# Block-sparse attention and a Fourier mixer on one core: another order of table loads and last stores, and one round of the second channel layer as seven block products

## The chip, the core and the metric

The kernel runs on one core of a Trainium2 chip. A core has five engines that run side by side, each with its own instruction stream: TensorE (PE) multiplies matrices from SBUF into PSUM, VectorE (DVE) and ScalarE (ACT) work on tiles elementwise, GpSimd (POOL) does the same more slowly, and SyncE (SP) here does little but issue DMA transfers, in its order. Data is held in SBUF (128 partitions); products land in PSUM, which has 8 banks. The engines meet by semaphores: an instruction whose input isn't there waits, and all that stands behind it on its engine waits with it.

The metric is the device time of one execution in microseconds (us). Of the kernel before, three runs are shown.

## The reference

The input has 4 batches, 8 heads, 768 positions and 64 numbers per head. The first part is attention with a mask by blocks of 32 positions: a block sees its neighbours, the first and last block, all blocks if it is itself the first or last, and three sampled ones.

```
scores = scale * q @ k.T                 # per batch and head, 768 x 768
scores = where(mask, scores, -1e9)
attn   = exp(scores - max) / (sum + 1e-9)
o      = attn @ v                        # 768 x 64
x      = o, heads side by side           # (4, 768, 512)
```

The second part mixes x by Fourier transforms and two channel layers:

```
u  = x + real(fft(fft(x, axis=1), axis=2))
un = (u - mean(u)) / sqrt(var(u) + 1e-6)
y  = u + relu(un @ w_ch1) @ w_ch2        # 512 -> 2048 -> 512
```

The weights arrive as float64; x and y are float32.

## The kernel before

All work is in float32. For each batch there are four pairs of heads (`NP` = 4), so 16 pairs in all. The work for a pair is cut into six steps called slots (`slot(sl)`, `SP` = 6); a phase is one batch's 24 slots (`SB` = 24), and there are 96 slots in all. In a slot, TensorE makes two tiles of scores (`scores`, L578: s, transposed, keys on partitions), ScalarE exponentiates them (`weigh`, L598 or L606), for the tiles whose mask is not made by TensorE VectorE multiplies by the mask (L608), and TensorE multiplies by v one or two slots later (`values`, L652: o, transposed). The sums for the softmax are gathered on GpSimd and VectorE (L638). When the six slots of one half of the positions are through, `place` transposes the result (xt, L673 to L676: three TensorE transposes and one copy by ScalarE) into x, or `place_blocks` sends it through HBM. x has two halves, xA and xB (384 positions each: tiles 0 to 2 and 3 to 5 of 128), with two buffers each, so batch b's x takes the buffer of batch b-2: it can't be written before b-2's result, which lies there, has been stored.

Which position lies in which partition of which tile is given by the table `_ORDER`: each row names a tile, a first partition, how many tiles and rows, and the first position and its step. The loads of q, k and the sine table and the stores of the output follow it; one DMA is issued for each row.

The mixer of batch b-1 runs inside the attention of batch b; that of the last batch runs behind all attention. Its parts, in order: `fourier` folds x, multiplies by the cosine and sine tables of the positions (zp, L860) and then by those of the channels (`across`, pq, L891 to L908); `arrive` adds the result to x; `spread` takes mean and variance (VectorE's statistics L941, GpSimd's root L943 to L945); `whiten` makes un (L955). un is needed transposed: in batches 0 to 2 VectorE transposes blocks of 32 (`un_blocks`, L1014), the rows go to HBM (far<-un) and come back in another order (unT<-far, `fetch`, L1027); in the last batch TensorE transposes (`un_flip`, utp, L996).

The channel layers then run in rounds; four rounds of 512 hidden channels each for batches 0 to 2. A round has two calls of `quad`, which makes two strips of 128 hidden channels by two halves of positions with 7 block products instead of 8 (xp, yp and z at L1103; the combined operands `right`, L1065, and `left`, L1085; sums L1108; relu L1112; the hidden layer lies in hA and hB), and six calls of `channels`: for each half and each tile of 128 positions, four matmuls of 512 columns (y, L1159) and one addition into x (L1162). In the last round the finished x is stored (`store`, L1170). The last batch has two rounds of 1024 hidden channels, in each four quads and then `outputs` for the tiles in the order `OUT`: tile m of xA and tile m of xB are made together by 7 block products (yy, L1224) with sums of operands (`output_left`, `output_right`) and additions (L1231, L1254).

The order of all this is written by a planner in Python that runs before the kernel does. It keeps a model clock for each engine (`when`, moved on by `busy(engine, us, after)`) and for each PSUM bank (`free`). Work that belongs to attention is emitted by `slot`; the mixer's steps wait in queues: `apart` (the Fourier part, normalisation, operands of the first quad), `late` (quads and channels, each with a price in us) and `short` (small TensorE steps that need one bank). `gap` emits from `apart` what the model clocks say fits in now. `until(met)` emits `late` and `apart` until a condition holds; it is used where x's buffer must be free (`finished` holds the halves whose stores have been issued) and at the end, for the last batch. In `slot`, for the first pair of a phase from phase 2 on (`reuse`), the place of the first half stands at step s >= 5 and first calls `until` for batch b-2's half; the placing itself is emitted in the next slot behind its scores and exponentials (`state["place"]`).

At the start the weights are loaded in 32 pieces (`w_load`, L456, by SP) and rebuilt from float64 by two ScalarE and five VectorE instructions each (`w_round`, L465 to L477). Six steps for the Fourier tables are spread over the slots by `table_step`: each step loads a table into one of two buffers (tab, L391 for the positions' tables) and later copies it in its final order with VectorE (L397). From slot 4 on, every even slot loads one and, from the third on, first copies out the oldest:

```
if len(table_put) == 2 or not table_steps:
    if table_put:
        table_put.popleft()()
if table_steps:
    fn, args = table_steps.pop(0)
    get, put = fn(*args)
    get()
    table_put.append(put)
```

A second version of the whole kernel (`general`) stands behind a condition for scores too large to be exponentiated without their maximum; it is not executed with these inputs.

## Time and profile before

| what | us |
|---|---|
| median of 3 runs | 1051.01 (1050.29 to 1051.64) |
| the profiled execution | 1051.83 |
| its span, first to last instruction | 1049.9 |
| TensorE busy | 1022.6 (97%) |
| VectorE busy | 672.5 (64%) |
| ScalarE busy | 356.2 (34%) |
| GpSimd busy | 236.6 (23%) |
| mean granted clock of TensorE | 0.994 of full speed |

How to read the rows of the profile. Times are us from the start of the span. In a row of the timeline stand the start, the duration, the engine, the line of the kernel, the operation, the output and inputs with partitions x elements, and how many like instructions were joined in the row; a bracket at the end gives the idle time ahead of it and what ended that. "SPq" is SP's queue for issuing DMAs and "ACTq" that of ScalarE; a DMA row's duration is the time for issuing, not for the transfer. A float32 matmul is recorded as two parts, so the x8 behind y stands for four matmuls. In a table by stretches of time, a row holds the stretch, its length, then busy time and count for PE, PEld, DVE, ACT and POOL, then the granted clock of TensorE, the mean busy share of the 16 DMA engines and the GB/s moved. In the chain of waits, a row names the waiting queue or engine, the one it waited for with the line, the time in all, how often and the longest.

### The profile page before, as it was taken

How to read it: one execution, taken by the hardware profiler on the slowest of the kernel's cores; microseconds unless marked ns; L12 is line 12 of the kernel's file. 1: busy time of each engine (PE TensorE's matmuls, PEld its weight loads, DVE VectorE, ACT ScalarE, POOL GpSimd, SP SyncE). 2: the span in 40 equal slices, each digit the busy share in tenths (PEclk: the TensorE clock that was granted, in tenths of full speed). 3: DMA queues.
4: the chain of work that ended last, by engine and by line, in shares of the span. 5: the costliest groups of instructions: out<-in, count | busy, mean ns of one | idle time of the engine just before them, and what ended most of it. 6: DMA issues, size and time to landing. Idle time of an engine off the chain costs nothing. (4 is left out here: it accounts for less than half of the span.)

```text
span 1049.9 us, 12342 instructions
## 1 busy us (share of the span) xinstructions
PE 1022.6 (97%) x4350; PEld 530.7 (51%) x4350; DVE 672.5 (64%) x1232; ACT 356.2 (34%) x718; POOL 236.6 (23%) x264
## 2 busy tenths in 40 slices
PE   8999999999999999999999999899999999999996
PEld 4333345444465554444444654444445654578585
DVE  6898885977845844655578467565558364774663
ACT  6979756554020112432441211243221111210210
POOL 1000074655000100554553001256420001000000
PEclk9999999999999999999999999999999999999998
DMA  7757522282000035232220003721010001000001
GB/s 212 227 180 216 121 47 46 51 140 37 1 1 20 31 40 87 62 64 39 56 58 1 1 10 74 124 53 42 16 25 7 0 1 39 22 1 1 1 17 46
DMA packets 163455, 58.05 MB, mean 55 GB/s; under 512 B 144172, under 2 KB 154170, under 8 KB 163386
## 3 DMA queue, kind: packets, MB, share of 16 engines
q1 hardware_dynamic: 162134, 56.45, 24.1%
q10 hardware_dynamic: 1220, 0.72, 0.3%
q8 instruction: 36, 0.59, 0.2%
q14 instruction: 33, 0.27, 0.1%
q0 software_dynamic: 32, 0.01, 0.0%
HBM read 43.80 MB, written 13.37 MB: 54 GB/s over the span
## 5 line engine op out<-in xcount | busy, mean ns | idle before, releaser
L638 POOL TENSOR_TENSOR acc<-acc,e 128x384 f32<-128x384 f32 x156 | 159.2, 1054 | 90.6 <-DVE e L608 68.2
L578 PE MATMUL s<-qT,kT 64*128 64x384 f32 x768 | 154.0, 515 | 9.8 <-ACT e L598 8.4
L652 PE MATMUL o<-e,vr 128*64 128x384 f32 x768 | 142.9, 499 | 0.0
L1159 PE MATMUL y<-w_sb,hB 128*128 128x512 f32 x288 | 128.1, 595 | 0.3 <-DVE x L1162 0.3
L1159 PE MATMUL y<-w_sb,hA 128*128 128x512 f32 x288 | 127.9, 595 | 0.0
L1162 DVE TENSOR_TENSOR x<-y,x 128x512 f32<-128x512 f32 x72 | 49.7, 690 | 113.8 <-PE y L1159 113.4
L608 DVE TENSOR_TENSOR e<-s,mask 128x768 f32<-128x768 f32 x84 | 76.3, 950 | 54.5 <-ACT s L606 46.3
L578 PEld LDWEIGHTS s<-qT,kT 64*128 64x128 f32 x768 | 63.7, 185 | 90.6 <-ACT e L598 29.0
L638 POOL TENSOR_TENSOR acc<-e 128x384 f32<-128x384 f32 x42 | 48.0, 1164 | 249.7 <-ACT e L598 125.6
L606 ACT ACTIVATE s<-s 128x768 f32<-128x768 f32 x84 | 63.6, 792 | 113.9 <-PE s L578 113.7
L598 ACT ACTIVATE e<-s 128x768 f32<-128x768 f32 x108 | 82.6, 812 | 56.0 <-PE s L588 35.0
L1103 PE MATMUL z<-unT,t 128*128 128x384 f32 x256 | 93.5, 488 | 0.0
L1159 PEld LDWEIGHTS y<-w_sb,hB 128*128 128x128 f32 x288 | 53.4, 190 | 66.5 <-issue 65.2
L1159 PEld LDWEIGHTS y<-w_sb,hA 128*128 128x128 f32 x288 | 53.7, 190 | 63.7 <-issue 60.0
L652 PEld LDWEIGHTS o<-e,vr 128*64 128x64 f32 x768 | 48.0, 137 | 69.7 <-issue 67.8
L1108 DVE TENSOR_TENSOR hA<-z,hA 128x384 f32<-128x384 f32 x64 | 35.7, 557 | 71.6 <-PE z L1103 71.5
L1112 ACT ACTIVATE hA<-hA 128x384 f32<-128x384 f32 x64 | 33.4, 523 | 123.6 <-DVE hA L1108 123.6
L1103 PEld LDWEIGHTS z<-unT,t 128*128 128x128 f32 x256 | 49.1, 192 | 34.4 <-issue 0.9
L1112 ACT ACTIVATE hB<-hB 128x384 f32<-128x384 f32 x64 | 33.5, 523 | 88.6 <-DVE hB L1108 88.6
L1123 ACT COPY hA<-xp 128x384 f32<-128x384 f32 x32 | 15.3, 477 | 123.3 <-PE xp L1103 123.3
L1103 PE MATMUL z<-t,w_sb 128*128 128x384 f32 x128 | 46.7, 488 | 2.8 <-DVE t L1065 2.8
L1103 PE MATMUL z<-t,t 128*128 128x384 f32 x128 | 47.8, 497 | 0.0
(208 smaller groups left out, 1372.5 us busy)
## 6 DMA issues: line engine op xcount, KB each, us to landing
wraw<-in_moe_w_ch_dram SPq DMA_DIRECT2D x32, 512.0 KB
vr<-in_v_dram SPq DMA_DIRECT2D x30, 192.0 KB
far<-un SPq DMA_DIRECT2D x18, 256.0 KB
unT<-far SPq DMA_DIRECT2D x24, 192.0 KB
qb<-in_q_dram SPq DMA_DIRECT2D x44, 96.0 KB
kb<-in_k_dram SPq DMA_DIRECT2D x44, 96.0 KB
out_dram<-x SPq DMA_DIRECT2D x11, 252.0 KB
out_dram<-x SPq DMA_DIRECT2D x18, 128.0 KB
```

The costliest lines, as they stand in the source:

```text
L578: nc.tensor.matmul(s[:, i, 0:HS], kT[rows, c * P:(c + 1) * P], qT[rows, queries], start=True, stop=u not in by_pe)
L598: nc.scalar.activation(out=e, in_=s[:, :, 0:HS], func=ACT.Exp, scale=scale)
L606: nc.scalar.activation(out=s[:, :, 0:HS], in_=s[:, :, 0:HS], func=ACT.Exp, scale=scale)
L608: nc.vector.tensor_tensor(out=e, in0=s[:, :, 0:HS], in1=m.broadcast_to([P, 2, HS]), op=ALU.mult)
L638: nc.gpsimd.tensor_add(out=acc[:, i, :], in0=start[:, i, :], in1=e[:, i, :])
L652: nc.tensor.matmul(o[D * i:D * i + D, :], vt[:, i, c, :], e[:, i, :], start=(c == 0), stop=(c == C - 1))
L1103: nc.tensor.matmul(to, a[:, k, :], c[:, k, :], start=(k == 0), stop=(k == ND // 2 - 1))
L1108: tt(out=to, in0=ps, in1=a, op=ALU.add)
L1112: nc.scalar.activation(out=h, in_=h, func=ACT.Relu)
L1123: nc.scalar.copy(out=h11, in_=x)
L1159: nc.tensor.matmul(y, hs[0, half][:, l, m * P:(m + 1) * P], w2_sb[:, 4 * r + l, :], start=(l == 0), stop=(l == 3))
L1162: nc.vector.tensor_tensor(out=x[:, m, :], in0=y, in1=x[:, m, :], op=ALU.add)
```

## The change

Six edits.

1. In `_ORDER`, the row of tile 5 with 63 rows becomes two with 48 and 15 rows, and the sine table's load, which follows it, too.
2. The tables' loads and copies come at slots named one by one: two loads (4, 5), two rounds of copies (8, 9), two loads (11, 12), and so on, and no longer at every even slot.
3. A round of the second channel layer that begins in `until(..., alone=True)`, which is the call behind all attention, and is not the batch's last, is made by `round_of`: for each tile m, xA's and xB's rows together by 7 block products of 256 columns (yz, yw and yc are their PSUM tiles) and not by two times four matmuls of 512 columns. The weights' differences (`round_right`) are made by GpSimd, the sums of the hidden layer (`round_left`) by VectorE and GpSimd, and three products of each tile are copied out by ScalarE (`keep`) and added by GpSimd (`later`). For these sums it takes the four tiles of the exponentials (`sums_room`), after attention's last values have been emitted (`drain`). In this kernel one round qualifies: round 2 (of 0 to 3) of batch 2.
4. The last batch takes its tiles in the order `OUT` = 0, 1, 2 and no longer 2, 0, 1. A half counts as finished when three tiles of it have been stored.
5. The first half's place in phases 2 and 3 stands at step 4, and no longer at step 5, while channel steps are left in `late`.
6. In the planner: `gap` takes a bound on the start of a step (`start`, given behind the seven products), the surcharge in `behind` is smaller beyond attention, and `do_apart` emits a pending `total` ahead of a TensorE step once a half has been finished.

```
-          (5, 0, 1, 0, 1, 512, 1), (5, 1, 1, 0, 63, 386, 2), (5, 64, 1, 0, 64, 385, 2))
+          (5, 0, 1, 0, 1, 512, 1), (5, 1, 1, 0, 48, 386, 2), (5, 49, 1, 0, 15, 482, 2),
+          (5, 64, 1, 0, 64, 385, 2))
...
-                rows = [(0, 1, src[P:P + 1, :]), (1, 63, src[2:P:2, :]), (64, 64, src[1:P:2, :])]
+                rows = [(0, 1, src[P:P + 1, :]), (1, 48, src[2:98:2, :]),
+                        (49, 15, src[98:P:2, :]), (64, 64, src[1:P:2, :])]
...
-    def table_step():
-
-        if len(table_put) == 2 or not table_steps:
-            if table_put:
-                table_put.popleft()()
-        if table_steps:
+    TABLES = {4: "g", 5: "g", 8: "p", 9: "p", 11: "g", 12: "g", 14: "p", 15: "p",
+              17: "g", 18: "g", 20: "p", 21: "p"}
+
+    def table_step(sl):
+
+        if TABLES.get(sl) == "p":
+            table_put.popleft()()
+        elif sl in TABLES:
...
+            if not last:
+                if p % 2 == 0:
+                    seven[p // 2] = state["alone"] and p // 2 < NF // 4 - 1
+                elif seven[p // 2]:
+                    state["drain"]()
+                    sums_room()
+                    for j in (1, 2, 4, 3):
+                        round_right(p // 2, j)
...
+        def round_right(r, j):
+            a, c = {1: (part(r, 0, 1), part(r, 0, 0)), 2: (part(r, 1, 1), w_t[1]),
+                    3: (part(r, 1, 1), part(r, 0, 1)), 4: (part(r, 1, 0), w_t[2])}[j]
+            nc.gpsimd.tensor_tensor(out=w_t[j], in0=a, in1=c, op=ALU.subtract)
+            busy("POOL", 1.35)
...
+        def round_of(r, m):
...
+            c_at, at = ps_m.tile([P, 512], FP32, tag="m", name="yc")[:, 0:DH], bank("m")
+            a_at = plus(a0, c_at, product(c_at, a12, part(r, 1, 0), True))
+            give(at, a_at - HOP)
+            k0 = keep(0, u_at, product(u_at, a11, part(r, 0, 0), True, z_at[0]))
+            later(a0, 0, max(a_at, k0))
+            o_at, at = ps_m.tile([P, 512], FP32, tag="m", name="yc")[:, 0:DH], bank("m")
+            give(at, plus(b0, o_at, product(o_at, a22, w_t[4], True)) - HOP)
+            if m == OUT[0]:
+                round_left(m, 3)
+                round_left(m, 4)
+            gap(start=0.9)
+            k1 = keep(1, u_at, product(u_at, a21, w_t[2], False, k0))
+            later(a1, 1, k1)
+            k2 = keep(2, d_at, product(d_at, h_s[1], w_t[1], True, z_at[1]))
+            done = product(u_at, h_s[3], w_t[3], False, k1)
+            tt(out=both, in0=both,
+               in1=u_at.rearrange("p (o d) -> p o d", o=1).broadcast_to([P, 2, DH]), op=ALU.add)
+            z_at[0] = busy("DVE", 0.7, done) + HOP
+            later(b1, 2, max(z_at[0], k2))
+            z_at[1] = plus(a1, d_at, product(d_at, h_s[4], part(r, 1, 1), False, k2))
+            ahead(1, 2, 3, 4)
+            state["soon"] = 1.6
...
         def channels(r, half, m):
 
+            if seven.get(r):
+                round_of(r, m)
...
-        OUT = (2, 0, 1)
+        stored = [0, 0]
         last = b == B - 1
+        OUT = (0, 1, 2) if last else (2, 0, 1)
...
-        if s >= (5 if reuse else 3) and (n, 0) in oT_at and once(n):
+        if s >= ((4 if late else 5) if reuse else 3) and (n, 0) in oT_at and once(n):
...
-        if sl >= 4 and sl % 2 == 0:
-            table_step()
+        table_step(sl)
...
-    until(lambda: len(finished) == 2 * B)
+    state["drain"] = lambda: None
+    until(lambda: len(finished) == 2 * B, True)
```

More of the change, by code (lines that the diff above doesn't have):

```diff
@@ L179 @@
     sum_p = ctx.enter_context(tc.tile_pool(name="sum_p", bufs=1))
+    wt_p = ctx.enter_context(tc.tile_pool(name="wt_p", bufs=1))
     big = ctx.enter_context(tc.tile_pool(name="big", bufs=1))
@@ L1153, in quad, with sums_room, cut @@
                     output_right(p // 4, j, p // 2 % 2)
-        def channels(r, half, m):
+            elif p % 2 == 1 and seven[p // 2]:
+                state["soon"] = 0.4
+        seven = {}
+        w_t, h_s, kept = {}, {}, {}
+        def sums_room():
+            def cut(t, at, k):
+                return t[:, at:at + 2 * HS // 3 * k].rearrange("p (k n) -> p k n", k=k)
+            rooms = [ep.tile([P, 2 * HS], FP32, tag="e", name="of") for _ in range(4)]
+            w_t[1] = wt_p.tile([P, 2, DH], FP32, tag="wt", name="wt")
+            for t, j in zip(rooms, (2, 3, 4)):
+                w_t[j] = t[:, 0:2 * DH].rearrange("p (k n) -> p k n", n=DH)
+            for t, j in zip(rooms, (1, 3, 4)):
+                h_s[j] = t[:, 2 * DH:2 * HS].rearrange("p (k n) -> p k n", n=P)
+            for i in range(3):
+                kept[i] = rooms[3][:, i * DH:(i + 1) * DH]
@@ new lines, in part, with tokens @@
+        def part(r, k, n):
+            return w2_sb[:, 4 * r + 2 * k:4 * r + 2 * k + 2, n * DH:n * DH + DH]
+        def round_right(r, j):
[3 more added lines that the diff above has]
+            busy("POOL", 1.35)
+        def tokens(m):
+            return [hs[0, i][:, 2 * k:2 * k + 2, m * P:(m + 1) * P]
+                    for i in range(2) for k in range(2)]
@@ new lines, in round_left @@
+        def round_left(m, j):
+            a11, a12, a21, a22 = tokens(m)
+            to, a, c, op = {1: (h_s[1], a21, a22, ALU.add), 2: (a21, h_s[1], a11, ALU.subtract),
+                            3: (h_s[3], a22, a21, ALU.subtract),
+                            4: (h_s[4], a12, a21, ALU.subtract)}[j]
+            if j > 2:
+                nc.gpsimd.tensor_tensor(out=to, in0=a, in1=c, op=op)
+                busy("POOL", 0.75, when["DVE"])
+            else:
+                tt(out=to, in0=a, in1=c, op=op)
+                busy("DVE", 0.43)
@@ new lines, in round_of, with product, keep, plus @@
+        def round_of(r, m):
+            after = dict(zip(OUT, OUT[1:])).get(m)
+            a11, a12, a21, a22 = tokens(m)
+            a0, a1 = xA[:, m, 0:DH], xA[:, m, DH:DM]
+            b0, b1 = xB[:, m, 0:DH], xB[:, m, DH:DM]
+            both = xB[:, m, :].rearrange("p (n d) -> p n d", n=2)
+            u_at, d_at = (ps_s.tile([P, 2, 512], FP32, tag="s", name=name)[:, 0, 0:DH]
+                          for name in ("yz", "yw"))
+            def product(to, a, c, start, after=0.0):
+                for k in range(2):
+                    nc.tensor.matmul(to, a[:, k, :], c[:, k, :], start=start and k == 0,
+                                     stop=k == 1, skip_group_check=True)
+                return busy("PE", 0.87, after) + HOP
+            def keep(i, src, done):
+                nc.scalar.copy(out=kept[i], in_=src)
+                return busy("ACT", 0.36, done) + HOP
+            def plus(to, src, done):
+                tt(out=to, in0=src, in1=to, op=ALU.add)
+                return busy("DVE", 0.43, done) + HOP
+            def later(to, i, at):
+                nc.gpsimd.tensor_add(out=to, in0=kept[i], in1=to)
+                busy("POOL", 0.75, at)
+            def ahead(*js):
+                if after is not None:
+                    for j in js:
+                        round_left(after, j)
+            if m == OUT[0]:
+                round_left(m, 1)
+                round_left(m, 2)
+            c_at, at = ps_m.tile([P, 512], FP32, tag="m", name="yc")[:, 0:DH], bank("m")
[5 more added lines that the diff above has]
+            give(at, plus(b0, o_at, product(o_at, a22, w_t[4], True)) - HOP)
+            if m == OUT[0]:
+                round_left(m, 3)
[12 more added lines that the diff above has]
+            state["soon"] = 1.6
@@ L1157, in channels @@
+        def channels(r, half, m):
+            if seven.get(r):
+                round_of(r, m)
+                if m == OUT[-1]:
+                    for _ in range(T):
+                        late.popleft()
+                return
             y, at = ps_m.tile([P, DM], FP32, tag="m", name="y"), bank("m")
@@ L1170, in store @@
                 queue.dma_start(out=rows, in_=x[p0:p0 + cnt, m, cols])
-            if m == out_of[half][-1]:
+            if cols.stop == DM:
+                stored[half] += 1
+            if stored[half] == T:
                 finished.add((b, half))
+        stored = [0, 0]
         last = b == B - 1
-        OUT = (2, 0, 1)
+        OUT = (0, 1, 2) if last else (2, 0, 1)
         out_of = (OUT, OUT if last else (0, 1, 2))
@@ L1328 @@
     state = {"paired": False, "total": None, "w": 0, "got": 0, "owed": 0.0, "ready": 0.0,
-             "back": 0.0, "place": None}
+             "back": 0.0, "place": None,
+             "alone": False, "drain": lambda: None}
     def channel_step():
@@ L1337, in behind @@
         at = max(when["DVE"], state["ready"])
-        return 0.75 * (len(kind) - 1) if when["POOL"] > at else 0.0
+        return (0.25 if state["alone"] else 0.75) * (len(kind) - 1) if when["POOL"] > at else 0.0
     def do_apart():
         kind, fn, pe, act, dve, _ = apart.popleft()
+        if finished and kind[0] in "mt" and state["total"] in short:
+            short.remove(state["total"])
+            state["total"][2]()
         if kind[0] in "dwb":
@@ L1359, in do_apart, with gap @@
         state["ready"] = done
-    def gap(rest=0.0, ahead=None, kinds="tm"):
+    def gap(rest=0.0, ahead=None, kinds="tm", start=None):
         used = "".join(k for k in "tm" if k not in kinds)
@@ L1374, in gap @@
                     break
-                if max(when["DVE"], state["ready"]) + dve > when["PE"] + rest + ahead:
+                at = max(when["DVE"], state["ready"]) - when["PE"]
+                if at + dve > rest + ahead if start is None else at > start:
                     break
@@ L1389, in gap, with until @@
                 fn()
-    def until(met):
+    def until(met, alone=False):
+        state["alone"] = alone
         while not met():
@@ L1395, in until @@
                 channel_step()
-                gap(2.0)
+                soon = state.pop("soon", None)
+                gap(2.0, start=soon)
             else:
                 do_apart()
+        state["alone"] = False
     def begin(b):
@@ L1484, in slot, with drain @@
             load_k(n + 1)
+        def drain():
+            while due:
+                sum_up()
+        state["drain"] = drain
         reuse = n % NP == 0 and phase >= 2
-        if s >= (5 if reuse else 3) and (n, 0) in oT_at and once(n):
+        if s >= ((4 if late else 5) if reuse else 3) and (n, 0) in oT_at and once(n):
             b, j = pairs[n]
```

## The prediction

> **What bounds the kernel now.** I read the page first, then the chain of waits, TensorE's waits, and the timeline around each place where TensorE stood idle.

> ```profile
> PE 1022.6 (97%) x4350; PEld 530.7 (51%) x4350; DVE 672.5 (64%) x1232; ACT 356.2 (34%) x718; POOL 236.6 (23%) x264
> ...
> PE 34%; DVE 1%; DMA 1%; SPq 0%; issue 0%; ACT 0%; DVEq 0%
> ```

> TensorE is busy for 97% of the span and carries nearly all that the chain holds. So a change gains in three ways only: less TensorE work, fewer of the 27 us (1049.9 less 1022.6) in which it idles, or a shorter stretch behind its last product. The change reaches two of its longest idle stretches inside the run. First:

> ```profile
> SPq L391 <- DVE cs_sb L397: 11.1, 2, 7.9
> ...
> 47.60 3.31 SPq L456 DMA_DIRECT2D wraw<-in_moe_w_ch_dram  x2
> ...
> 58.27 0.63 DVE L397 COPY cs_sb<-tab 128x128 f32<-128x128 f32 x5
> ...
> 58.93 1.17 SPq L391 DMA_DIRECT2D tab<-in_sin_s_dram  x3
> ...
> 64.16 1.50 SPq L456 DMA_DIRECT2D wraw<-in_moe_w_ch_dram  x3
> ...
> 68.45 0.66 ACT L465 ACTIVATE wraw<-wraw 128x512 f32<-128x512 uint32 x1 [3.12 <-DMA wraw<-in_moe_w_ch_dram]
> ...
> 70.42 1.78 PE L578 MATMUL s<-qT,kT 64*128 64x384 f32 x8 [2.24 <-ACT e L598]
> ```

> ```profile
> 70.00:72.00 2.00, 1.58 (x10) 0.72 (x12) 1.90 (x4) 2.00 (x5) 0.00 (x0) 0.93 0.87 179
> 72.00:74.00 2.00, 2.00 (x11) 0.94 (x9) 1.93 (x5) 2.00 (x5) 0.00 (x0) 0.50 0.84 299
> 74.00:76.00 2.00, 2.00 (x12) 0.63 (x12) 1.90 (x4) 2.00 (x5) 0.00 (x0) 0.71 1.10 320
> ...
> 672.00:674.00 2.00, 2.00 (x5) 1.13 (x5) 1.82 (x3) 0.03 (x1) 0.00 (x0) 0.62 0.41 86
> 674.00:676.00 2.00, 2.00 (x4) 1.07 (x4) 0.72 (x2) 0.49 (x1) 0.00 (x0) 0.53 0.41 67
> ```

> SP issues nothing from 50.9 to 58.9: the third table load needs a room that is freed by the copies of the first (58.27), which VectorE reaches late. So the weight loads behind it start at 64.16, ScalarE waits 3.12 us for one in order, and TensorE 2.24 us for ScalarE's exponential. In the second table of rows the column after POOL is the granted clock: after this stall it averages 0.93, 0.50 and 0.71 over three stretches of 2 us, which loses 2 x (0.07 + 0.50 + 0.29) = 1.7 us more. Second:

> ```profile
> 650.78 4.08 SPq L1027 DMA_DIRECT2D unT<-far  x4
> ...
> 652.27 1.50 ACT L606 ACTIVATE s<-s 128x768 f32<-128x768 f32 x2 [13.48 <-PE s L578]
> ...
> 653.79 1.82 DVE L608 TENSOR_TENSOR e<-s,mask 128x768 f32<-128x768 f32 x2
> 654.25 0.55 PE L675 MATMUL xt<-ident,oT 128*128 128x128 f32 x3
> ...
> 654.90 2.05 SPq L1170 DMA_DIRECT2D out_dram<-x  x2
> 656.16 1.56 PE L578 MATMUL s<-qT,kT 64*128 64x384 f32 x8
> ...
> 659.56 0.48 ACT L676 COPY x<-xt 128x384 f32<-128x384 f32 x1 [5.79 <-DMA out_dram<-x]
> 659.94 0.85 ACT L535 ACTIVATE qT<-qb 128x768 f32<-128x768 f32 x1
> ...
> 671.12 1.56 PE L1103 MATMUL z<-t,w_sb 128*128 128x384 f32 x4 [2.77 <-DVE t L1065]
> ```

> At 671.12 the first pair of channel layer 1 waits 2.77 us for operands that came back through HBM. The clock then falls again (0.62 and 0.53, 1.7 us lost): 4.5 us in all. Mark ScalarE at 659.56: its copy of the attention output into x waits 5.79 us until batch 1's rows, which lay there, are stored (654.90 and on); everything behind it on ScalarE waits too. TensorE does not feel it, since its next scores (656.16) use the tiles that were weighed at 652.27 and 653.79, ahead of the copy.

> **The change, part by part.** The sum is made against the profiled execution (1051.83 us with a span of 1049.9); the median of the runs, 1051.01, is 0.82 lower, and I subtract the sum from that.

> *Tables.* Two loads, then two rounds of copies, so that SP asks for a third room three slots after the copies that free it. The same loads and copies are issued; the sine load of 63 rows becomes two (48 and 15), one issue more on SP, about 0.5 us (654.90: two issues in 2.05 is the dearest row, 58.93: three in 1.17 the cheapest), at a time when SP has 8 us free. The copies are moved past weight rounds on VectorE, 0.63 us a set. The attention of batch 0 on TensorE hides both; were VectorE to lag more, the PSUM banks that it empties would come free late and TensorE would wait for them. Bounds: nothing gained; or 2.24 + 1.7 = 3.9. I take 3.9, because nothing else kept SP from issuing.

> *Attention place one slot earlier (batches 2 and 3).* While channel work is left, the planner finishes batch b-2's first half at step 4 of a pair and no longer at 5. In TensorE's order the scores of step 5 move from ahead of that block to behind it, and the transposes xt and their ScalarE copy move ahead of the next scores. For batch 3 the new order is: y of hA (12 products), scores, xt, y of hB (4), scores, o (8), scores. Everything of the block comes 1.5 us earlier (one set of scores, as the row at 656.16), the last store of the first half too: SP issues it after the four unT loads, 654.90 - 1.5 = 653.4, and it lands at 659.5 - 1.5 = 658.0. ScalarE reaches the copy at 648.8 and now stands 9 us, with the next exponentials behind it. TensorE wants the tiles of those exponentials at about 656.0 (the old 656.16: the work ahead of it is the same). They are free after the copy (0.45), the squares of kb (0.85 + 0.19, as the row at 659.94), one exponential (0.75) and one mask product (0.91, half of 653.79's): 658.0 + 3.3 with the hand-overs = 661.3. A stall of 5.3 us, where there was none. The old stall at 671.12 almost closes, since TensorE arrives later: 0.2 left. With one fall of the clock at the same 1.7: 5.3 + 0.2 + 1.7 = 7.2 against 4.5 before, a loss of 2.7. Bounds: ScalarE is not held, then the operands' 1.5 us come off the old stall and no fall of the clock follows: -1.5 - 1.7 = -3.2; the clock stays low twice as long: +4.4. For batch 2 the same move is harmless by this row:

> ```profile
> 410.72 0.48 ACT L676 COPY x<-xt 128x384 f32<-128x384 f32 x1 [1.05 <-PE xt L675]
> ...
> 412.05 1.56 PE L578 MATMUL s<-qT,kT 64*128 64x384 f32 x8
> ```

> There the copy waited 1.05 us, for TensorE alone, so the store was in by then; 1.5 less is 409.2 at the latest, with 3.3 behind it 412.5 against scores asked for at 412.05. So at most 0.5; I take 0, as the store may have been in long before; the end above is what a hold like batch 3's would cost (rivals).

> *Seven products.* Only one round qualifies: it begins beyond the attention and is not the last of batch 2. Six products of 4 matmuls of 512 columns become 3 x 7 products of 2 matmuls of 256.

> ```profile
> 838.26 6.87 PE y L1159 x16
> ...
> 1004.00 36.37 PE yy L1224 x168
> ```

> A record is half a matmul: 6.87 us for 8 matmuls, 36.37 for 84. Removed: 24 x 0.859 = 20.6. Added: 42 x 0.433 = 18.2. Gain 2.4. Beside it lie, on ScalarE, 9 copies of 256 columns (a 384-wide one takes 0.48, row 659.56), on VectorE 12 sums of 256 columns, 6 left operands and 3 sums of 512 in place of 6 of 512 (0.69 and 0.42, rows below), on GpSimd 4 differences of weights, 6 of tokens, 9 sums. VectorE and GpSimd have room in this stage; each copy has one product, 0.87, as cover for about 0.65 of hand-over, copy and hand-back. Without that cover each would cost what it exceeds. GpSimd's memset of zs now stands behind two of its differences, ScalarE's copy of zs behind the memset, and a kept copy behind that: I allow 0.5. Then the order of the end of batch 2 changes: the third frequency product (pq, 2.1) moves behind the first y of the last round, and with it what follows on VectorE.

> ```profile
> 885.06 0.69 DVE L941 BATCH_NORM_STATS2 st<-x 128x6 f32<-128x512 f32 x1
> ...
> 886.05 0.42 POOL L943 TENSOR_SCALAR st<-st 128x1 f32<-128x1 f32 x1 [2.80 <-DVE st L942]
> ...
> 886.55 0.56 POOL L945 TENSOR_TENSOR st<-st,neg_half 128x1 f32<-128x1 f32 x1
> ...
> 889.07 3.70 PE L1159 MATMUL y<-w_sb,hB 128*128 128x512 f32 x8 [0.35 <-DVE x L1162]
> ...
> 892.81 0.69 DVE L1162 TENSOR_TENSOR x<-y,x 128x512 f32<-128x512 f32 x1 [3.79 <-PE y L1159]
> 893.42 0.54 DVE L955 TENSOR_SCALAR un<-x,st 128x512 f32<-128x512 f32 x1
> ...
> 894.01 0.66 PE L996 MATMUL utp<-ident,un 128*128 128x128 f32 x4 [0.80 <-DVE un L955]
> ...
> 897.33 1.56 PE L1103 MATMUL z<-t,w_sb 128*128 128x384 f32 x4
> ```

> Before, the last whitening (893.42) directly follows the last y's sum and the next quad's z starts at 897.33, 4.8 us behind the last y (892.5). After, one statistics pair, GpSimd's root and two whitenings stand behind that sum: 0.2 + 0.69 + 0.87 + 1.1 + 0.54, so the last whitening ends 3.4 us behind the last y, the transposes and the four-fold differences follow, and z starts at 7.1. Of the 2.3 later, 0.9 are two transposes that moved there; the 0.35 idle at 889.07 goes. Net 1.0 lost. Together: -2.4 + 0.5 + 1.0 = -0.9, with bounds -2.4 (all covered) and +2.

> *Last stores.* Tokens 2 come last and no longer tokens 1.

> ```profile
> 1038.12 1.90 ACTq L1170 DMA_DIRECT2D out_dram<-x  x3
> ...
> 1040.39 0.42 DVE L1231 TENSOR_TENSOR x<-yy,x 128x256 f32<-128x256 f32 x1 [0.97 <-PE yy L1224]
> ...
> 1043.00:1044.00 1.00, 0.00 (x0) 0.00 (x0) 0.00 (x0) 0.00 (x0) 0.00 (x0) 1.00 0.69 168
> ...
> 1046.00:1047.00 1.00, 0.00 (x0) 0.00 (x0) 0.00 (x0) 0.00 (x0) 0.00 (x0) 0.50 0.14 49
> 1047.00:1048.00 1.00, 0.00 (x0) 0.00 (x0) 0.00 (x0) 0.00 (x0) 0.00 (x0) 0.50 0.07 25
> ```

> The end is a store of 2 x 63 rows (tile 4) that runs at 46 to 49 GB/s with a DMA share of 0.14, two of 16 engines, behind an equal one of ScalarE's queue; it ends about 1047.7, 7 us after the last product. After, tile 5 takes that place in four stores (48 and 15 for 63) that use more engines, and a 2 x 63 of tile 2 is issued last, at 1041.3 behind the sum of 1040.39. ScalarE's equal store is issued by 1040.0 and done at about 1044, when the traffic falls to 46 GB/s and one stream: 4 us. The new last one, issued by 1042.0 with a store of one row behind it, then ends at 1046 to 1046.5: -1.3. Bounds 0 and -2.3 (126 KB at 47 GB/s take 2.7, so no less than 1045.4 with 0.7 to start).

> Sum: -3.9 + 2.7 + 0 - 0.9 - 1.3 = -3.4. 1051.0 - 3.4 = 1047.6; by its own bounds 1045.5 to 1050. The two added copies of the mask's set-up (one row more in the order table) are under 0.2.

> **Rivals.** *ScalarE is not held in batch 3* because the store lands before its copy: -3.9 - 3.2 - 0.9 - 1.3 = -9.3, 1041.7. Against it: the 5.79 at 659.56 shows that this copy waits even in its later place. *The tables gain nothing*, another wait takes the place of SP's: 0 + 2.7 - 0.9 - 1.3 = +0.5, 1051.5. Against it: the whole wait goes back to SP's, row by row. [...] *Slower*: the hold strikes batch 2 as well, where the store must land later than 408 for TensorE to feel it; at batch 3's price, 5.3 + 1.7 = 7.0, the sum is +3.6, 1054.6. It decides from 5.6 us on. For it: same order of instructions; against it: 410.72 waited 1.05 us for TensorE and for no store. *Slower too*: the seven products' copies aren't covered; at 0.65 for each of 9 the sum is -3.4 + 5.9 = +2.5, 1053.5.

> **Numbers.** Forecast 0.50, ScalarE not held 0.20, tables nothing 0.10, clock 0.08, the two slower ones 0.07 and 0.05. A difference of 0.2%, 2.1 us, is about what a measurement of this kernel can tell from none: faster ends at 1048.9. Of the forecast I count 0.38 as faster and 0.12 as same. Faster 0.58, same 0.30, slower 0.12. The range reaches to the first rival and past the second: 1041 to 1052.

> **What the changed profile would show.** Right: no wait of SP for cs_sb, no ScalarE wait for wraw, clock full at 70 to 76; scores waiting some 5 us near 655 in phase 4 behind a ScalarE copy that waits for out_dram; yz, yw and yc with no idle ahead; some 7 us (4.8 before) between the last y of batch 2 and the first z of batch 3; the last store ending about 5.5 us behind the last product. Wrong: scores without a wait there (then 1042), a stall of the same kind near 410 (then 1054), or TensorE idle ahead of yz (the copies).

## The result and the profile after

The changed kernel takes 1045.55 us in the median (1045.29 to 1047.49), against 1050.65 of the kernel before (1049.45 to 1051.95): a ratio of 0.9954, interval 0.9943 to 0.9966. That is 5.1 us less, where the prediction had 3.4 less and 1047.6. The time lies in its range and the sign is right. But the sum holds errors of opposite sign, as the profile shows: that it came this close is in part luck. The first rows of the page of after, then rows of TensorE's waits, of after and of before:

```profile
span 1043.6 us, 12498 instructions
PE 1018.6 (98%) x4382; PEld 537.0 (51%) x4382; DVE 683.2 (65%) x1246; ACT 359.3 (34%) x727; POOL 257.7 (25%) x287
```

```profile
PE s L583 <- DVE e L613: 5.4, 2, 4.5
PE s L583 <- ACT e L603: 3.9, 10, 0.9
PE z L1116 <- DVE t L1070: 1.5, 2, 1.3
```

```profile
PE s L578 <- ACT e L598: 8.4, 13, 2.2
PE z L1103 <- DVE t L1065: 2.8, 1, 2.8
PE s L578 <- DVE e L608: 1.1, 2, 0.8
```

TensorE is busy 4.0 us less and idle 2.3 us less. The wait of scores for ScalarE's exponentials fell from 8.4 to 3.9 us; a wait for VectorE's e, 4.5 us at one place, is new. To see where the time went, the start of the same TensorE instruction was read in both traces, at points where nothing is in another order:

```
point                                      before    after    shift
attention of batch 0, ahead of the stall    61.20    61.42    +0.21
attention of batch 0, behind it             83.69    79.96    -3.73
attention, ahead of batch 2's channel work 238.62   235.14    -3.49
attention, behind it                       454.67   447.54    -7.13
attention, ahead of batch 3's channel work 546.99   539.87    -7.13
attention, behind it                       680.99   677.81    -3.18
alone, ahead of the seven products         811.47   808.29    -3.18
batch 3, second quad                       903.88   899.00    -4.88
last product, its end                     1040.35  1035.46    -4.89
end of the span                           1049.9   1043.6     -6.3
```

So in these two executions: tables 3.9 less, batch 2's block 3.6 less, batch 3's block 4.0 more, the seven products 1.7 less, the last stores 1.4 less (the rest, 0.4, are shifts of 0.2 at the start and in batch 1). The rows behind the first and third, from the timeline of after (70 us, then 650 us), with a table by stretches of the same place (the column behind the five engines is the granted clock):

```profile
70.00:72.00 2.00, 2.00 (x15) 0.80 (x11) 1.90 (x5) 2.00 (x4) 0.00 (x0) 1.00 0.87 278
72.00:74.00 2.00, 2.00 (x18) 0.94 (x18) 1.93 (x5) 2.00 (x4) 0.00 (x0) 1.00 0.68 168
```

```profile
650.26 0.48 ACT L681 COPY x<-xt 128x384 f32<-128x384 f32 x1 [8.70 <-DMA far<-un]
650.64 0.85 ACT L540 ACTIVATE kb<-kb 128x768 f32<-128x768 f32 x1
...
651.48 1.50 ACT L611 ACTIVATE s<-s 128x768 f32<-128x768 f32 x2
652.31 1.82 DVE L613 TENSOR_TENSOR e<-s,mask 128x768 f32<-128x768 f32 x2 [3.91 <-ACT s L611]
...
653.32 2.93 PE L583 MATMUL s<-qT,kT 64*128 64x384 f32 x8 [4.52 <-DVE e L613]
```

```profile
652.32:655.73 3.41, 2.41 (x8) 1.14 (x8) 1.81 (x2) 2.58 (x5) 0.00 (x0) 0.50 1.01 138
655.73:659.15 3.42, 3.42 (x6) 1.42 (x5) 2.80 (x3) 0.88 (x2) 0.00 (x0) 0.50 1.17 114
```

At 70 us there is no wait and no half clock any more. At 653.32 stands the stall that was predicted for batch 3, with the chain as predicted: copy, squares of kb, exponential, mask product, scores. The profile names far<-un as what ScalarE waited for. But ScalarE's own waiting instructions, in the view of the copy's line, are these:

```profile
L681 ACTq EVENT_SEMAPHORE  x4: 17/38/38, 649.7 to 650.2; - x4
```

The first of them carry the semaphores of the two stores of out_dram, which landed from 649.3 to 650.0; far<-un landed from 650.2 to 650.6, when the last of these waits was ending. So the store is what it waited for.

### The profile page after: what moved, and what is told of

It is laid out like the page before. It is cut to its first block, busy times and chain, and to the rows that moved or that the text cites. A ratio compares the mean times of both kernels' runs of the same rounds, so it can differ in the third digit from the quotient of the medians.

```text
span 1043.6 us, 12498 instructions
## 1 busy us (share of the span) xinstructions
PE 1018.6 (98%) x4382; PEld 537.0 (51%) x4382; DVE 683.2 (65%) x1246; ACT 359.3 (34%) x727; POOL 257.7 (25%) x287
## 4 chain that ended last, share of the span: by engine, by line
PE 84%; DVE 8%; DMA 2%; ACT 2%; SPq 2%; issue 1%; ACTq 0%; DVEq 0%
PE y L1281 20%; PE z L1116 16%; PE s L583 11%; PE o L657 9%; PE yp L1116 8%; PE yy L1349 7%; PE xp L1116 4%; PE zp L865 2%; PE sp L728 1%; PE s L593 1%; DMA far<-un 1%; ACT e L603 1%; DVE t L1070 1%; PE yz L1224 1%; DVE acc L638 1%
## 5 line engine op out<-in xcount | busy, mean ns | idle before, releaser
L643 POOL TENSOR_TENSOR acc<-acc,e 128x384 f32<-128x384 f32 x160 | 163.4, 1054 | 126.3 <-DVE e L613 106.7
L1281 PE MATMUL y<-w_sb,hB 128*128 128x512 f32 x264 | 118.9, 601 | 0.0
L1281 PE MATMUL y<-w_sb,hA 128*128 128x512 f32 x264 | 117.1, 595 | 0.0
L1284 DVE TENSOR_TENSOR x<-y,x 128x512 f32<-128x512 f32 x66 | 45.6, 691 | 98.3 <-PE y L1281 98.1
L1281 PEld LDWEIGHTS y<-w_sb,hB 128*128 128x128 f32 x264 | 49.6, 192 | 62.0 <-issue 61.3
L1281 PEld LDWEIGHTS y<-w_sb,hA 128*128 128x128 f32 x264 | 49.2, 190 | 59.5 <-issue 55.7
L1116 PE MATMUL xp<-unT,w_sb 128*128 128x384 f32 x128 | 47.2, 492 | 0.0
```

The costliest lines, as they stand in the source:

```text
L643: nc.gpsimd.tensor_add(out=acc[:, i, :], in0=start[:, i, :], in1=e[:, i, :])
L1116: nc.tensor.matmul(to, a[:, k, :], c[:, k, :], start=(k == 0), stop=(k == ND // 2 - 1))
L1281: nc.tensor.matmul(y, hs[0, half][:, l, m * P:(m + 1) * P], w2_sb[:, 4 * r + l, :], start=(l == 0), stop=(l == 3))
L1284: nc.vector.tensor_tensor(out=x[:, m, :], in0=y, in1=x[:, m, :], op=ALU.add)
```

## The experiments

All comparisons are with runs of the kernel before on the same chip. First each suspected part by itself.

**Tables alone.** The kernel before with the new slots (`TABLES`), nothing else.

```
+    TABLES = {4: "g", 5: "g", 8: "p", 9: "p", 11: "g", 12: "g", 14: "p", 15: "p", ...
-        if sl >= 4 and sl % 2 == 0:
-            table_step()
+        table_step(sl)
```

> The kernel before with the new slots for table loads and copies alone. If the whole step near 70 us comes from the order of the tables (theory): 3.7 us less than before, near 1047.0, no weight load of SP held behind a table load, clock full from 70 to 76 us, and nothing changed behind 90 us. If another edit took part (rival, the 48 and 15 rows make the sine load land sooner): less than 2 us.

Measured: 1047.27, ratio 0.9961 (0.9946 to 0.9976), 3.5 less. In its trace the clock also falls at another place: it is 0.50 from 244.03 to 247.44, behind the waits at the head of batch 2's block, and 1.00 from 672 to 676, where it fell before. The expectation that nothing changes behind 90 us was wrong in that. The reverse, the changed kernel with the old slots:

```
-    TABLES = {4: "g", 5: "g", 8: "p", 9: "p", 11: "g", 12: "g", ...
+    TABLES = {4: "g", 6: "g", 8: "pg", 10: "pg", 12: "pg", 14: "pg", 16: "p", 18: "p"}
...
```

> The changed kernel with the old slots for the tables. Theory: SP is held again behind the third table load, the wait and the fall of the clock near 70 us come back: 3.7 us more, near 1049.2. Rival (what the start loses is hidden later, since TensorE waits elsewhere for transfers): less than 2 more.

Measured: 1050.73, ratio 0.9998 (0.9987 to 1.0009): all of the gain is gone, 5.2 us, and it is 1.5 above the expected 1049.2. By the trace's shift it is 3.9 behind 70 us and 3.4 at the end; its clock falls again at 71.1. The other 1.6 of the 5.0 between the two spans lie behind the last product, where the stores are the same in both kernels: one of the last stores took SP 1.54 us to issue here and 0.48 in the changed kernel. Why is not shown; the tables have no part in it that the trace shows. By the trace, then, the step is worth 3.4 here, as in the kernel before (3.5), and what the start loses is not hidden later.

**Place at step 4 alone**, in both batches, in the kernel before.

```
-        if s >= (5 if reuse else 3) and ...
+        if s >= ((4 if late else 5) if reuse else 3) and ...
```

> The kernel before with the place at step 4 alone, in batches 2 and 3. Theory after the result: two effects of nearly equal size. At the head of batch 2's block (240 us) a set of scores that waited goes behind the block, 3.3 us less, with some 0.3 at its end; in batch 3 ScalarE's copy is held and the clock falls for longer, 3.9 more: together +0.3, 1050.4 to 1051.4. The prediction's own step (nothing in batch 2, +2.7 in batch 3) gives 1053.4. If the gain at 240 us belongs to another edit (rival): about 1054.5.

Measured: 1051.74, ratio 1.0004 (0.9996 to 1.0013), 0.3 above the expected interval: no difference, made of two. In its trace, attention behind batch 2's block starts 3.2 us earlier than before and behind batch 3's block 3.1 us later again. The prediction's own step (nothing and +2.7) is excluded. What went at batch 2's block are these rows of the kernel before, at the head of the block and not at its end, where the prediction looked:

```profile
242.03 1.51 PE L652 MATMUL o<-e,vr 128*64 128x384 f32 x8
243.28 2.66 POOL L638 TENSOR_TENSOR acc<-e 128x384 f32<-128x384 f32 x2
243.35 0.81 ACT L598 ACTIVATE e<-s 128x768 f32<-128x768 f32 x1 [2.17 <-POOL acc L638]
...
244.22 0.92 PE L578 MATMUL s<-qT,kT 64*128 64x384 f32 x4 [0.67 <-ACT e L598]
...
245.97 0.81 ACT L598 ACTIVATE e<-s 128x768 f32<-128x768 f32 x1 [1.81 <-POOL acc L638]
...
246.84 0.92 PE L578 MATMUL s<-qT,kT 64*128 64x384 f32 x4 [1.71 <-ACT e L598]
247.59 0.49 PE L588 MATMUL s<-factors 64*128 64x384 bf16 x4
248.01 1.56 PE L1103 MATMUL xp<-unT,w_sb 128*128 128x384 f32 x4
```

The scores of step 5 wait here for exponentials, and these for GpSimd, which still sums the tiles that they would overwrite: 0.67 + 1.71 = 2.4 us of idle TensorE just ahead of 160 us of channel work that needs no exponentials. The place at step 4 calls for the whole block one slot earlier, so these scores go behind it. GpSimd then catches up under the channel work, and VectorE makes the mask in place of TensorE's 0.42 us (L588), as it does for all tiles behind the first channel step. In after, the same place reads:

```profile
238.39 1.51 PE L657 MATMUL o<-e,vr 128*64 128x384 f32 x8
239.07 3.38 POOL L643 TENSOR_TENSOR acc<-e 128x384 f32<-128x384 f32 x2
239.14 0.81 ACT L603 ACTIVATE e<-s 128x768 f32<-128x768 f32 x1 [1.96 <-POOL acc L643]
239.83 1.56 PE L1116 MATMUL xp<-unT,w_sb 128*128 128x384 f32 x4
```

ScalarE waits for GpSimd as before, but TensorE goes on with the first quad. At the block's end, where the prediction looked, the copy does wait for a store now, and no scores wait for it:

```profile
400.00 0.48 ACT L681 COPY x<-xt 128x384 f32<-128x384 f32 x1 [1.90 <-DMA out_dram<-x]
...
401.05 1.56 PE L583 MATMUL s<-qT,kT 64*128 64x384 f32 x8
```

**The same within the changed kernel.** Place at step 5 in both batches, then at step 4 in batch 2 alone; together with the changed kernel this prices each batch.

```
-        if s >= ((4 if late else 5) if reuse else 3) and ...
+        if s >= (5 if reuse else 3) and ...
```

> The changed kernel with the place at step 5 in both batches, as before the change. Theory: in batch 2 the scores stand ahead of the block again and wait there for exponentials (2.4 us in the trace of before, with the mask by TensorE 3.3 in all), in batch 3 nothing is held: 1039.1, the time with step 4 in batch 2 alone, plus 3.3: 1042.4; up to 1.7 more if the clock falls in one of the two places. Rival (the waits at 240 us went because the tables come earlier, not because of the move): 1039.1.

```
-        if s >= ((4 if late else 5) if reuse else 3) and ...
+        if s >= ((4 if late and phase == 2 else 5) if reuse else 3) and ...
```

> The changed kernel with the place at step 4 in batch 2 alone, at step 5 in batch 3 as before. Theory: batch 3's loss of 3.9 goes, its old stall of 2.8 and the fall of the clock come back with the old order: 1041.6. Rival (in the changed kernel batch 3's stall is there in either order, since all comes 7 us earlier and the stores with it): 1045.5.

Measured: 1043.14 (ratio 0.9936, 0.9922 to 0.9950) with step 5 in both; 1039.12 (0.9891, 0.9877 to 0.9905) with step 4 in batch 2 alone; 1045.55 with step 4 in both. So batch 2's move gains 4.0 us and batch 3's loses 6.4. Taken together edit 5 makes the changed kernel 2.4 us slower than it would be without it. The 6.4 is more than the 4.0 by the traces, and more than any theory had. Most of the rest is the clock. In the kernel before, z's wait in batch 3 (2.77 us) took a fall of the clock with it, 1.7 us more; with step 4 in batch 2 alone the same wait is 2.16 us long and takes none:

```profile
659.43:662.84 3.41, 1.87 (x6) 0.76 (x4) 1.46 (x3) 0.48 (x1) 1.51 (x2) 1.00 0.52 77
662.84:666.25 3.41, 2.78 (x9) 1.75 (x10) 3.33 (x5) 0.00 (x0) 0.00 (x0) 1.00 0.42 94
```

The granted clock stays 1.00 in both stretches, in which TensorE is idle for 1.54 (3.41 - 1.87) and 0.63 us; the mean of this execution is 0.997, and 0.994 in before. The last experiment looks at when it falls. The six runs with step 5 in both are of two kinds: three with a mean granted clock of 0.998 took 1041.84 to 1042.72, three with 0.994 to 0.996 took 1043.56 to 1045.88. Against the first three, batch 2's move gains 2.7 to 3.6.

**The copy held in batch 3.** The changed kernel, but in batch 3 `place` is emitted one slot later, behind the next exponentials; the block itself stays where the change put it.

```
-        if state["place"]:
+        if state["place"] and (phase < 3 or s != 5):
             state["place"]()
```

> The changed kernel, but in batch 3 the transposes xt and ScalarE's copy of them stand one slot later, behind the next exponentials; the block's end stays at step 4. Theory (ScalarE is held by the copy, and the next exponentials with it): no wait of scores near 653, no fall of the clock there, z waits at most 1.3 to 1.5: 3 to 5.8 us less than the changed kernel, 1040 to 1042.5. Rival (the scores are late for another reason, the mask products on VectorE or the operands of the next quad): the wait near 653 stays and the time with it, 1045.5.

Measured: 1039.07, ratio 0.9888 (0.9874 to 0.9903), 6.5 us less than the changed kernel, below the interval that was expected. Its timeline:

```profile
644.89 1.65 ACT L611 ACTIVATE s<-s 128x768 f32<-128x768 f32 x2 [2.79 <-PE s L583]
...
648.01 1.80 DVE L613 TENSOR_TENSOR e<-s,mask 128x768 f32<-128x768 f32 x2
649.01 1.78 PE L583 MATMUL s<-qT,kT 64*128 64x384 f32 x8
650.53 0.48 ACT L681 COPY x<-xt 128x384 f32<-128x384 f32 x1 [3.99 <-DMA far<-un]
```

The copy still waits, until the same time (650.5 against 650.3), but the exponentials stand ahead of it, and the scores at 649.01 follow without a wait. That one instruction of ScalarE, by its place in the order, costs the whole stall and the fall of the clock: the mean granted clock is 0.997 here and 0.994 in the changed kernel (TensorE's three transposes xt move with it; they have no wait at this place in either trace). The rival, late mask products or operands, is out.

**Seven products.** The changed kernel with the round made by y products, and the end of batch 2 in the old order.

```
-                    seven[p // 2] = state["alone"] and p // 2 < NF // 4 - 1
+                    seven[p // 2] = False
```

> The changed kernel without the seven products (every round by y products of 512 columns, the end of batch 2 in the old order). Theory (the shift between the two traces grows by 1.7 over this stage): 1.7 us more than the changed kernel, near 1047.3. The prediction's sum for this part was 0.9: 1046.4. If the products gain nothing at all in the median (rival: their gain of 2.4 is eaten by the later first quad of batch 3): 1045.5.

Measured: 1048.1, ratio 0.9981 (0.9971 to 0.9990): 2.6 us more than the changed kernel. By the trace, the shift over this stage is 1.7 (0.44 to 2.15). The stage in after and here:

```profile
819.70:842.70 23.00, 23.00 (x121) 19.89 (x120) 11.79 (x26) 5.85 (x17) 10.74 (x15) 1.00 0.00 1
```

```profile
821.00:847.00 26.00, 26.00 (x92) 14.06 (x91) 8.62 (x22) 2.25 (x8) 1.21 (x3) 1.00 0.00 1
```

TensorE has no idle time in either. The copies are covered, GpSimd's 10.7 us too. The 0.5 that the prediction allowed for a late zs did not come. Edit 6 of the change was not run by itself. It is in this version too, whose trace is 2.74 us earlier than that of the kernel before where the stage begins (811.47 there) and 2.73 where it ends (903.88). So without the seven products edit 6 shows no effect in this stage.

**Last stores.** The changed kernel with the old order of the last tiles; then with the new order, but tile 5's 63 rows in one store.

```
-        OUT = (0, 1, 2) if last else (2, 0, 1)
+        OUT = (2, 0, 1)
```

> The changed kernel with the last batch's tiles in the order 2, 0, 1, still with 48 and 15 rows for tile 5. The last stores are then 2 x 63 rows of tile 4 and of tile 1's partner again. Theory (the tail is set by which tile's 63-row stores come last): 1.4 us more, near 1046.9, the tail behind the last sum 9.5 and no longer 8.1. Rival (the rows of tile 5 are what helps): no change, 1045.5.

```
-          (5, 0, 1, 0, 1, 512, 1), (5, 1, 1, 0, 48, 386, 2), (5, 49, 1, 0, 15, 482, 2),
+          (5, 0, 1, 0, 1, 512, 1), (5, 1, 1, 0, 63, 386, 2),
```

> The changed kernel with tile 5's 63 rows stored by one DMA again, the order of tiles 0, 1, 2 kept. If the split is needed for the gain (the 63-row store of tile 5 uses fewer engines than 48 and 15 do): some 0.5 to 1.4 us more, tail 8.6 to 9.5. If the order of tiles alone carries it: within 0.3 us of the changed kernel, tail 8.1.

Measured: 1047.36 (ratio 0.9968, 0.9958 to 0.9979), 1.8 more, with the old order; 1045.17 (0.9949, 0.9936 to 0.9963), no difference, with 63 rows in one. So the order of the tiles carries the gain, and the split into 48 and 15 carries none of it. DMA issues of the last 16 us of the changed kernel, then of the one with the old order:

```profile
out_dram<-x SPq DMA_DIRECT2D x1, 126.0 KB
```

```profile
out_dram<-x ACTq DMA_DIRECT2D x1, 126.0 KB
out_dram<-x SPq DMA_DIRECT2D x1, 126.0 KB
```

With the old order, the last tiles are 1 and 4, and both halves of tile 4's columns leave as stores of 2 x 63 rows, 0.6 us apart, one behind the other. With the new one tile 2 has them, whose first half of columns is stored before its last products; only one is left at the end. The last stretches in after:

```profile
1036.00:1037.00 1.00, 0.00 (x0) 0.00 (x0) 0.00 (x0) 0.00 (x0) 0.00 (x0) 1.00 0.47 121
1038.00:1039.00 1.00, 0.00 (x0) 0.00 (x0) 0.00 (x0) 0.00 (x0) 0.00 (x0) 0.51 0.16 45
1041.00:1042.00 1.00, 0.00 (x0) 0.00 (x0) 0.00 (x0) 0.00 (x0) 0.00 (x0) 0.50 0.04 14
```

From 1038 on it still runs at 45 GB/s with a DMA share of 0.16, and its data is out 5.8 us behind the last product (1041.28 less 1035.46; before, 1047.71 less 1040.35 = 7.4). A share of 0.16 is that of two to three of 16 engines (0.16 x 16 = 2.6, an estimate); why this store has no more is not shown. The stretch from 1036 to 1037, behind the issue of the stores of 48, 15 and 64 rows, has 0.47. In the run with 63 rows in one the highest share of a slice of 0.4 us behind 1030 is 0.9, and 0.5 in after: no run shows that 63 rows use fewer engines than 48 and 15.

**A version that beats both.** The changed kernel with the later copy, one store for the 63 rows, and the large stores of the last tiles issued first.

```
...
+            by_size = (lambda row: -row[1]) if last and m == OUT[-1] else (lambda row: 0)
-            for p0, cnt, rows in _rows(out[b][:, cols], T * half + m):
+            for p0, cnt, rows in sorted(_rows(out[b][:, cols], T * half + m), key=by_size):
...
+        if state["place"] and (phase < 3 or s != 5):
```

> The changed kernel with the later copy in batch 3, tile 5's 63 rows in one store, and in the last tiles the large stores issued ahead of the one-row ones. Theory: 1039.1 as with the later copy alone, and the tail shorter by the issue of one store, about 0.5: 1038.6; it is at most as long as with the later copy alone.

Measured: 1038.97, ratio 0.9889 (0.9875 to 0.9903): 1.1% less than before, 6.6 us less than the changed kernel. Beside the later copy alone (1039.07) the two small edits make no difference that can be measured.

**When the clock falls.** Work is added behind the changed kernel: groups of matmuls, each behind two to seven copies by ScalarE.

```
...
+        for i in range(42):
+            ps = ps_s.tile([P, 2, 512], FP32, tag="s", name="probe_ps")
+            for _ in range(16):
+                nc.tensor.matmul(ps[:, 0, 0:HS], ident, e[:, 0, :], start=True, stop=True)
+            for _ in range(2 + i % 6):
+                nc.scalar.copy(out=e[:, 0, :], in_=ps[:, 0, 0:HS])
...
```

> The changed kernel with work added behind it that the output doesn't need: 42 times 16 matmuls of 384 columns, each time behind two to seven copies by ScalarE, so that TensorE waits 1 to 4 us between groups. In the traces so far every fall of the clock starts at a whole multiple of 3.413 us from the first one of its trace. Theory (a fixed grid of windows of 3.413 us; a window with TensorE idle for some 2 us or more is followed by one at half clock): every fall lies on the grid, windows idle for more than 2.04 us are followed by a half one, those idle for less than 1.5 are not, and waits of equal length (2 to 3 us) go with a fall or without by how they lie to the grid. Rival (the length of a wait alone decides): all waits above one length are followed by a fall at their end, none below.

Two waits of TensorE in its timeline, 2.67 us and then 3.18:

```profile
1087.57 12.28 PE L1746 MATMUL probe_ps<-probe,ident 128*128 128x384 f32 x32 [2.67 <-ACT probe L1748]
...
1103.03 4.14 PE L1746 MATMUL probe_ps<-probe,ident 128*128 128x384 f32 x12 [3.18 <-ACT probe L1748]
```

and stretches of 3.413 us around them and around a third wait, the first of them ahead of a fall of the clock at 1087.63:

```profile
1084.22:1087.63 3.41, 0.74 (x4) 0.13 (x2) 0.00 (x0) 2.40 (x5) 0.00 (x0) 1.00 0.00 0
1087.63:1091.04 3.41, 3.41 (x6) 1.89 (x7) 0.00 (x0) 0.00 (x0) 0.00 (x0) 0.50 0.02 5
1097.87:1101.29 3.42, 1.98 (x7) 0.83 (x5) 0.00 (x0) 1.29 (x3) 0.00 (x0) 1.00 0.00 0
1101.29:1104.70 3.41, 1.67 (x5) 1.06 (x6) 0.00 (x0) 1.59 (x4) 0.00 (x0) 1.00 0.00 0
1104.70:1108.11 3.41, 3.41 (x12) 2.04 (x11) 0.00 (x0) 0.00 (x0) 0.00 (x0) 1.00 0.00 0
1152.49:1155.90 3.41, 1.25 (x5) 0.51 (x4) 0.00 (x0) 1.92 (x4) 0.00 (x0) 1.00 0.00 0
1155.90:1159.31 3.41, 3.41 (x6) 1.82 (x6) 0.00 (x0) 0.00 (x0) 0.00 (x0) 0.50 0.00 0
```

The shorter wait lies in one stretch, which is idle for 2.67, and the next one runs at half clock. The longer one lies across two, with 1.44 in the first and 1.74 in the second, and nothing follows. The stretch from 1152.49 is idle for 2.16, and the next one runs at half clock too; this fall is 68.27 us behind the one at 1087.63, which is 20 times 3.413. The rival, the wait's length alone, is out: 2.67 us had a fall and 3.18 had none.

## Why the prediction was right or wrong, point by point

In us; the shifts are from the two traces, the medians from what each part does when it is taken out of the changed kernel (for batch 2, step 5 in both against step 4 in batch 2 alone).

| step | predicted | shift in the traces | medians |
|---|---|---|---|
| tables | -3.9 | -3.9 | -5.2 (-3.5 when put into before) |
| place, batch 2 | 0 | -3.6 | -4.0 |
| place, batch 3 | +2.7 | +4.0 | +6.4 |
| seven products | -0.9 | -1.7 | -2.6 |
| last stores | -1.3 | -1.4 | -1.8 |
| sum | -3.4 | -6.3 | measured -5.1 |

The medians of the parts don't add up to the whole exactly (-7.2 against -5.1). Those of before alone reach from 1047.8 to 1053.4 in these runs, each part moves later waits, which had a fall of the clock in one kernel and none in another (z's wait in batch 3: 2.77 us with one in before, 2.16 without with step 4 in batch 2 alone), and 1.6 of the 5.2 for the tables lie behind the last product in the one trace that there is of it.

*Tables.* Right in mechanism and size: SP's wait, ScalarE's wait for weights and the fall of the clock all went, and came back with the old slots.

*Place in batch 2, "I take 0".* The step that failed. The prediction followed the moved scores to their new place at the block's end and asked what they would meet there, and was right that they meet nothing: ScalarE's copy waits 1.90 us and TensorE feels nothing. It didn't ask what they leave. They left a stall of 2.4 us and TensorE's own mask products (0.42) at the block's head, 2.8 of the 3.6 us. The waits for L598, 8.4 us in 13 places, stood in TensorE's waits, and the tables account for only 2.24 of them. The rival that was tied to this place (hold in batch 2, 1054.6) went the wrong way altogether.

*Place in batch 3.* Right in mechanism, at each link: ScalarE stands 8.70 us (predicted 9), the chain behind the copy's start takes 653.32 - 650.26 = 3.1 (3.3), the stall is 4.52 (5.3). Two sizes were off. The wait of z kept 1.30 (0.2 was allowed), and the clock stayed at 0.50 for 6.83 us instead of 3.41 (652.32 to 659.15), the upper end of this step's bounds. "ScalarE is not held" was not what happened here, though it describes the version with the later copy: 1039.07, where that rival had 1041.7.

*Seven products.* Right in mechanism. The gain of 2.4 came whole: the round takes 22.8 us (819.93 to 842.75) and before 26.4 (823.11 to 849.51), of which 1.1 is the frequency product that moved, so 2.5. The first z of batch 3 is 6.8 us behind the last y of batch 2 (7.1 predicted; 892.45 less 885.63), and the stages behind the round lose 0.8 (1.0 predicted). The term that was mis-sized is zs: 0.5 allowed, 0 measured, as TensorE is busy for all of the stretch. In the median the part is worth 2.6; the prediction had 0.9.

*Last stores.* Right in size, and half right in reason: two stores of 2 x 63 rows, one behind the other, became one. That 48 and 15 rows "use more engines" than 63 played no part: 1045.17 with 63 in one, 1045.55 with 48 and 15.

*The clock.* The prediction priced each fall at 1.7 and let every wait of 2.2 us and more have one. The price holds for one stretch of 3.41 us at 0.50, as before has two of; in after there were two in a row, 3.4 us lost. But not every such wait had a fall: z's wait in batch 3 cost 2.2 us with step 4 in batch 2 alone and 2.8 + 1.7 = 4.5 in before, and in the probe 3.18 us across two stretches had none. Nor was a whole idle stretch needed: ahead of the two falls in before TensorE was idle for 2.10 and 2.05 of 3.41 us, about 60%.

## What to carry to other kernels

When an instruction moves, look at both ends: what it meets in its new place, and whether it left a stall in the old one. An engine's copy that waits for a transfer holds all that stands behind it; move it behind the next work that a busier engine needs, which here was worth 6.5 us, more than the 5.1 of the whole change. A short stall of TensorE had two prices here, with and without a fall of the clock (4.5 and 2.2 us for z's wait), and a part's worth of a few us can't be read off a single pair of traces.

## What the runs showed of the hardware that was not expected

```profile
68.32:71.73 3.41, 1.31 (x8) 0.70 (x10) 2.45 (x9) 3.28 (x7) 0.00 (x0) 1.00 0.95 279
71.74:75.15 3.41, 3.41 (x15) 1.41 (x13) 3.27 (x7) 3.41 (x7) 0.00 (x0) 0.50 0.86 305
75.15:78.56 3.41, 3.41 (x26) 1.18 (x24) 3.24 (x7) 2.00 (x5) 0.00 (x0) 1.00 0.89 251
242.40:245.81 3.41, 2.06 (x12) 0.59 (x8) 2.52 (x3) 0.81 (x1) 3.41 (x3) 1.00 0.02 2
245.82:249.23 3.41, 2.39 (x12) 1.33 (x13) 2.42 (x3) 2.03 (x3) 0.40 (x2) 1.00 0.00 0
669.07:672.48 3.41, 1.36 (x4) 0.87 (x5) 3.38 (x4) 0.00 (x0) 0.00 (x0) 1.00 0.30 74
672.49:675.89 3.40, 3.40 (x7) 1.89 (x6) 1.94 (x5) 0.52 (x1) 0.00 (x0) 0.50 0.44 80
675.90:679.31 3.41, 3.41 (x11) 1.79 (x10) 2.18 (x5) 0.90 (x2) 0.00 (x0) 1.00 0.43 90
```

and of after, around its fall inside the run:

```profile
648.90:652.31 3.41, 0.00 (x0) 0.00 (x0) 0.00 (x1) 2.05 (x5) 0.00 (x0) 1.00 0.53 189
652.32:655.73 3.41, 2.41 (x8) 1.14 (x8) 1.81 (x2) 2.58 (x5) 0.00 (x0) 0.50 1.01 138
655.73:659.14 3.41, 3.41 (x6) 1.41 (x5) 2.80 (x3) 0.88 (x2) 0.00 (x0) 0.50 1.17 114
659.15:662.56 3.41, 3.41 (x14) 1.09 (x14) 1.01 (x2) 0.00 (x0) 0.36 (x1) 1.00 0.37 79
```

At full clock, stretches in which TensorE was idle for 2.10 and 2.05 us (before), 2.67 and 2.16 (probe) and all 3.41 (after) were followed by one at half clock; those with 1.35 and 1.02 (before), 1.44 and 1.74 (probe) were not, nor was the one with 1.54 in the run with step 4 in batch 2 alone. At half clock, the one with 1.00 idle (after) was followed by a second; those with none (before, after) were not. These rows show nothing of what lies between 1.74 and 2.05 us, nor of the first 7 us, and other kernels were not measured. The falls lie differently to the start of the program: the first at 71.74 us in before and the one at 652.32 in after are 580.58 us apart, 170.1 times 3.413. This may be a reason why executions of one kernel differ by some us, as the six with step 5 in both batches do (1041.84 to 1045.88 us at a mean granted clock of 0.998 to 0.994); that was not tested by itself.
